# Shared PSUM copies in tiles of their own, and two tap units ahead of the filter's rows, in an SSM convolution with a dense layer

## The chip, the cores and the metric

The kernel runs on one core of one Trainium2 chip. The metric is the device time of one execution in microseconds (us). An execution is also profiled: the trace lists each instruction with its engine, start and duration, and its span runs from the first to the last instruction. The engines are TensorE (PE: matmuls; PEld: its weight loads), VectorE (DVE), ScalarE (ACT), GpSimd (POOL) and SyncE (SP), which only issues transfers. ScalarE issues transfers too, on a queue of its own.

## What is computed

S is 2048 tokens, D is 512 channels, the hidden width is 1376. Cut to what matters:

```python
def _A_ref(q, k, v, shift_k, ssm_k, ssm_D):
    k_pad = jnp.pad(k, ((0, 0), (ks - 1, 0), (0, 0)))
    for t in range(ks):                       # ks = 4 taps per channel
        k_shift = k_shift + k_pad[:, t:t + S, :] * shift_k[:, ks - 1 - t][None, None, :]
    kv = k_shift * v
    y = irfft(rfft(kv, 2S) * rfft(ssm_k, 2S))[:S]       # a long convolution per channel
    y = y + kv * ssm_D
    return q * y

h = x + _A_ref(_layernorm(x), A_k, A_v, A_shift_k, A_ssm_k, A_ssm_D)
h2 = h + relu(_layernorm(h) @ B_w1) @ B_w2
```

## The kernel before

The long convolution is done as a transform in stages of matmuls, of the filter ssm_k and of kv, a product of the two, and the inverse. Then come the gate with q, the layer norm and the dense layer. Everything is written out by hand: each engine executes its instructions in the order of the program, and a helper derives the semaphores. The stages are these.

- **Loads.** SyncE issues the shift weights (wsh, L123), the whole filter ssm_k of 2 MB (tile sk, L124), and then for four pieces of 512 tokens the transposing loads of k and v, k first (L132 to L137). They follow each other in one queue.
- **Fill.** 22 matmuls on zeros (L156) keep TensorE busy until data is there.
- **Tables.** GpSimd makes ramps (iota), two identities (ident in bf16, identw in f32) and a mask; VectorE turns ramps into angles (`_turns`, L44 and L46; tsn, L222 and L220); ScalarE takes sines. ScalarE also makes 16 diagonal matrices wdiag from ident and the shift weights (L204): a matmul with one is a tap. VectorE makes the tables f1hi and f1lo of the first stage (L210 to L215).
- **Rows of the filter.** `to_rows` (L271 to L284) transposes sk on TensorE, 32 transposes in four groups of eight, and copies each group from PSUM into kfl: groups 0 and 2 by ScalarE, group 1 by VectorE, group 3 half by each engine (L281, L283), both from one PSUM tile.
- **Stage 1 of the filter** (`stage1`, L286 to L309): per call 32 pairs of weight load and small matmul into two PSUM tiles. VectorE adds the mask to a half of each (L306) and ScalarE copies the other half (L309).
- **Tap units** (`taps(c, h)`, L329 to L337): eight matmuls with diagonals give the shifted k of 512 tokens and two of the four channel groups; VectorE multiplies by v (L337). One unit stands behind each of the stage calls 0 to 5, two ahead of call 6.
- **Rows of kv** by `to_rows` again, the last stage call of the filter, and eight calls of stage 1 for kv, evicted by both engines (L267, L269).
- **Products** (L425 to L442), and the **inverse** (`inv1`, L550 to L562): 16 blocks of 12 matmuls, each evicted by two copies. ScalarE does most blocks, VectorE blocks 6, 8, 10, 12 and 14, and block 15 is shared half and half, from one PSUM tile. Then `inv2` (L634) writes pz, which the gate reads.
- **The dense layer** (`mlp1`, L646 and L648; `mlp2`, L659 to L665): four groups of four token tiles. Each token tile ends in one product on VectorE (L662) and a store that ScalarE issues (L665).

PSUM tiles of the first stages come in turn from four buffers of two banks each (`bank2`): a tile waits until the one four places before it has been read. A tile that two engines read has its readers ordered one behind the other.

Of the kernel before, what the change touches and what calls it, by code (L numbers as in the profile page):

```python
# [56 lines left out]
def kernel(  # L57
# [64 lines left out]
    wsh = consts.tile([P, DC, KS], BF16, name="wsh")  # L122
    nc.sync.dma_start(out=wsh[:], in_=A_shift_k.rearrange("(r p) j -> p r j", p=P))  # L123
    nc.sync.dma_start(out=sk, in_=A_ssm_k.rearrange("(c p) t -> p c t", p=P))  # L124
    draw = small([DC * P], BF16)
# [14 lines left out]
    nbias = consts.tile([P, 1], F32, name="nbias")  # L140
    pbias = consts.tile([P, 1], F32, name="pbias")
    nc.vector.memset(nbias[:], -0.5 * TURN)
    nc.vector.memset(pbias[:], 0.5 * TURN)
# [13 lines left out]

    fill(bank2("psz")[:, 0, :], 22)

    n1i = early.tile([P, 1], I32, name="n1i")  # L160
    for s in range(0, P, 32):
        nc.gpsimd.iota(n1i[s:s + 32, :], pattern=[[0, 1]], base=0, channel_multiplier=1)
    n2i = consts.tile([P, 1], I32, name="n2i")
    for s in range(0, P, 64):
        nc.gpsimd.iota(n2i[s:s + 64, :], pattern=[[0, 1]], base=0, channel_multiplier=1)
# [4 lines left out]
    f1hi = early.tile([P, 2, 2, 16, 2], BF16, name="f1_hi")  # L170
    f1lo = early.tile([P, 2, 2, 16, 2], BF16, name="f1_lo")
    for f in (f1hi, f1lo):
        nc.gpsimd.memset(f[:], 0.0)
    ident = early.tile([P, P], BF16, name="ident")
    identw = early.tile([P, P], F32, name="identw")
    for t in (identw, ident):
        nc.gpsimd.memset(t[:], 0.0)
        nc.gpsimd.affine_select(out=t[:], in_=t[:], compare_op=ALU.not_equal, fill=1.0,
                                base=0, pattern=[[-1, P]], channel_multiplier=1)
    nc.gpsimd.iota(r2, pattern=[[2, 32], [128, 64]], base=1, channel_multiplier=0)  # L180
    pi4 = consts.tile([P, 2], I32, name="pi4")
# [3 lines left out]
    nc.gpsimd.tensor_copy(out=rows4[:], in_=rows4[:].bitcast(I32))  # L185
    n1c = early.tile([P, 1], F32, name="n1c")
    n2c = consts.tile([P, 1], F32, name="n2c")
    nc.vector.tensor_copy(out=n1c[:], in_=n1i[:])
    nc.vector.tensor_copy(out=n2c[:], in_=n2i[:])
    wf = early.tile([P, DC, KS], F32, name="wf")  # L190
    nc.vector.tensor_copy(out=wf[:], in_=wsh[:])
    t1 = small([64], I32)
    _turns(nc, t1[:, 0:32], r1[:], n1c[:], 128, True)
# [7 lines left out]
    _sin(f1f[:, 32:64], t1[:, 32:64], 128, neg=True)  # L201
    for rg in range(DC):
        for j in range(KS):
            nc.scalar.mul(out=wdiag[:, rg, j, :], in_=ident[:], mul=wf[:, rg, j:j + 1])  # L204
    dsc = small([2, 64], F32)
    dpm = small([2, 64], F32)
    _sin(dsc[:], t3[:], 64)

    f1h = small([64], BF16)
# [7 lines left out]
    st = stp.tile([P, 32, 192], F32R, name="st")  # L217
    def wrap13(t):

        nc.vector.tensor_scalar(out=t, in0=t, scalar1=19, scalar2=19, op0=ALU.logical_shift_left, op1=ALU.arith_shift_right)  # L220

    nc.vector.tensor_single_scalar(out=tsn, in_=r2, scalar=n2c[:], op=ALU.mult)  # L222
    wrap13(tsn)

# [46 lines left out]
    def to_rows(src, h, fl):  # L271

        pst = bank2("pst").rearrange("p b (i c) -> p (b i) c", i=4)
        srcw = src.bitcast(F32).rearrange("p c (a w) -> p (c a) w", w=32)
        for i in range(8):
            nc.tensor.transpose(out=pst[:, i, :], in_=srcw[:, :, 8 * h + i], identity=identw[:])
        o = fl.bitcast(I32)
        for eng, i0, n in {0: (("A", 0, 8),), 1: (("D", 0, 8),), 2: (("A", 0, 8),), 3: (("A", 0, 4), ("D", 4, 4))}[h]:
            oi, pi = o[:, :, 8 * h + i0:8 * h + i0 + n], pst[:, i0:i0 + n, :]
            if eng == "A":  # L280
                nc.scalar.copy(out=oi.bitcast(F32), in_=pi.rearrange("p i c -> p c i"))  # L281
            else:
                nc.vector.tensor_single_scalar(out=oi, in_=pi.bitcast(I32).rearrange("p i c -> p c i"),  # L283
                                               scalar=0, op=ALU.bitwise_or)  # L284
# [43 lines left out]

    def taps(c, h, each=2):  # L329
        ps = bank2("pkv")  # L330
        for i in range(2):
            for j in range(KS):
                nc.tensor.matmul(out=ps[:, i, :], lhsT=wdiag[:, 2 * h + i, j, :],
                                 rhs=kT[c][:, 2 * h + i, 16 - j:CH + 16 - j], start=(j == 0), stop=(j == KS - 1))
        for i in range(0, 2, each):
            vv = vT[:, 2 * h + i:2 * h + i + each, CH * c:CH * c + CH]
            nc.vector.tensor_tensor(out=vv, in0=ps[:, i:i + each, :], in1=vv, op=ALU.mult)  # L337
# [196 lines left out]

    def inv1_mm(b, i, parts):
        g = 4 * b + i
        o = blocks[b][:, i].rearrange("p d a n -> p (d a n)")
        for part in parts:
            src = BX[:, 0] if part == 0 else BK[:, part - 1]
            rhs = inv3[:].rearrange("p d a n -> p (d a n)") if part == 0 else inv12[:, 4 - 2 * part:8 - 2 * part, :].rearrange("p a n -> p (a n)")  # L540
            nc.tensor.matmul(out=o, lhsT=src[:, g // 2, :, g % 2::2].rearrange("p c r -> p (c r)"), rhs=rhs,  # L541
                             start=(part == 0), stop=(part == 2), skip_group_check=True)
# [7 lines left out]
    def inv1(b, eng):  # L550
        if b in blocks:
            for i in range(4):
                inv1_mm(b, i, (0, 1, 2) if i % 2 else (1, 2))
        else:
            blocks[b] = bank2("psi").rearrange("p b (i d a n) -> p (b i) d a n", i=2, d=2, a=2)
            for i in range(4):
                inv1_mm(b, i, (0, 1, 2))
        ps = blocks[b]
        for e, i0, n in ((eng, 0, 4),) if len(eng) == 1 else ((eng[0], 0, 2), (eng[1], 2, 2)):
            for rho in range(2):  # L560
                copy(e, ax[rho][:, :, :, 8 * b + 2 * i0:8 * b + 2 * i0 + 2 * n],
                     ps[:, i0:i0 + n].rearrange("p i d a n -> p a n (i d)")[:, rho].rearrange("p (n m) c -> p n m c", m=2))  # L562

# [10 lines left out]
    for b in range(16):  # L574
        inv1(b, "AD" if b == 15 else "D" if b in (6, 8, 10, 12, 14) else "A")
        if b == 0:
            for n in range(4):
                center(n)
            ec_wrap(1)
            ln1_stats(0)  # L580
        if b == 3:
            ln1_norm(0)
        if b in (8, 9, 10, 11):
            ec_sins(1, (b - 8,))
        if b == 11:
            load_x(1)
# [65 lines left out]
    def mlp2(sc, hook=None):  # L652
        h1T = h1s[sc]
        for i in range(4):
            t = 4 * sc + i
            ps2 = psm.tile([P, D], F32, tag="ps", name="ps2m")
            for fc in range(NFC):
                ksz = min(P, DFF - fc * P)
                nc.tensor.matmul(out=ps2[:], lhsT=h1T[:ksz, fc, i * P:(i + 1) * P], rhs=w2[:ksz, fc, :],  # L659
                                 start=(fc == 0), stop=(fc == NFC - 1))  # L660
            o = ob[t % 3]
            nc.vector.scalar_tensor_tensor(out=o[:], in0=ps2[:], scalar=rstd2[:, t, :], in1=xh[sc][:, i, :],  # L662
                                           op0=ALU.mult, op1=ALU.add)
            dst = bass.AP(tensor=out_d.tensor, offset=out_d.offset + t * D, ap=[[16 * D, 4], [64 * D, 32], [1, D]])
            nc.scalar.dma_start(out=dst, in_=o)  # L665
            if hook is not None:
                hook(i)
# [76 lines left out]
```

## Time and profile before

| what | us |
|---|---|
| median of 3 runs (lowest, highest) | 214.96 (214.94, 216.5) |
| the profiled execution | 214.74 |
| its span | 213.0 |
| TensorE busy | 200.3 |
| VectorE busy | 141.2 |
| ScalarE busy | 115.7 |
| GpSimd busy | 70.3 |

The span is what the rows below cover; the rest of an execution's time lies outside. A row of the time line gives start, duration, engine, line, operation, output and inputs with shapes; in square brackets stand the engine's idle time before the row and what ended it. "SPq" and "ACTq" are transfers being issued: their duration is that of the issue, not of the transfer. A row of the waits gives the engine and line that waited, what it waited for, and us in total, number and longest. The row "PE" of digits divides the span into 40 slices of 5.3 us; a digit is the busy share in tenths.

### The profile page before, as it was taken

To read this page: it belongs to the slowest core of one execution; us is meant where nothing else is said; L and a number is where in the kernel's file an instruction comes from. 1 tells how busy PE (TensorE), PEld (TensorE's weight loads), DVE (VectorE), ACT (ScalarE), POOL (GpSimd) and SP (SyncE) were. 2 spreads that over 40 slices of the span, in tenths; PEclk is the share of its full clock that TensorE was granted. 3 is DMA by queue.
4 is the path that set the end of the run, shared out by engine and by line. 5 is a ranking of instruction groups with operands and counts; after the bars stand their busy time and mean duration, and the time that the engine had idled before them with its cause. 6 is when DMAs were issued, how large, how long until landed. Compare 5 with 4: busy or idle time off the path is not lost. (4 is left out here: it accounts for less than half of the span.)

```text
span 213.0 us, 4286 instructions
## 1 busy us (share of the span) xinstructions
PE 200.3 (94%) x1715; PEld 137.1 (64%) x1724; DVE 141.2 (66%) x243; ACT 115.7 (54%) x186; POOL 70.3 (33%) x119
## 2 busy tenths in 40 slices
PE   7779999999999999999997999999999999999990
PEld 2465555887888888789996954457444844444440
DVE  5978987599678887898743487897078742260121
ACT  3987776687777677657592039501970065026200
POOL 7954703995555893030103022420102110002000
PEclk9999999999999999999999999999999999999997
DMA  5999970001600000037315997999818715110011
GB/s 155 340 219 171 197 118 2 3 5 15 252 3 0 3 0 3 0 99 102 67 32 143 267 210 142 174 170 142 110 33 101 141 24 102 27 57 14 0 51 47
DMA packets 47686, 19.91 MB, mean 93 GB/s; under 512 B 42706, under 2 KB 46132, under 8 KB 47668
## 3 DMA queue, kind: packets, MB, share of 16 engines
q1 hardware_dynamic: 44144, 16.15, 41.1%
q10 hardware_dynamic: 3524, 3.51, 5.6%
q8 instruction: 13, 0.21, 0.5%
q14 instruction: 5, 0.04, 0.1%
HBM read 7.02 MB, written 2.10 MB: 43 GB/s over the span
## 5 line engine op out<-in xcount | busy, mean ns | idle before, releaser
L648 ACT ACTIVATE M<-ps1m 128x512 bf16<-128x512 f32 (+1 forms) x44 | 25.0, 601 | 49.9 <-PE ps1m L646 39.5
L659 PE MATMUL ps2m<-M 128*128 128x512 bf16 (+1 forms) x172 | 38.5, 379 | 0.2
L659 PEld LDWEIGHTS <-M 128*128 128x128 bf16 (+1 forms) x176 | 17.1, 98 | 20.9 <-ACT M L648 0.4
L646 PEld LDWEIGHTS <-w 128*128 128x128 bf16 (+1 forms) x176 | 17.4, 100 | 20.4 <-issue 0.7
L380 POOL TENSOR_TENSOR smc<-st 64x256 fp32r<-64x256 f32 x32 | 22.7, 729 | 11.1 <-PE us L435 10.2
L662 DVE SCALAR_TENSOR_TENSOR M<-ps2m,rstd,M 128x512 bf16<-128x512 f32 x12 | 9.0, 748 | 25.3 <-PE ps2m L659 16.8
L503 POOL TENSOR_SCALAR rstd<-mv 128x4 f32<-128x4 f32 x8 | 2.2, 276 | 70.9 <-DVE mv L501 70.9
L541 PE MATMUL psi<-inv,BK 128*128 128x256 f32 x128 | 22.7, 283 | 0.0
L442 DVE TENSOR_TENSOR BK<-u,ktu 128x512 fp32r<-128x512 f32 x32 | 20.4, 680 | 0.0
L541 PEld LDWEIGHTS psi<-inv,BK 128*128 128x128 f32 x128 | 19.9, 195 | 0.0
L646 PE MATMUL ps1m<-xT,w 128*128 128x512 bf16 (+1 forms) x88 | 19.6, 379 | 0.2 <-ACT M L648 0.2
L646 PE MATMUL ps1m<-M,w 128*128 128x512 bf16 (+1 forms) x88 | 19.3, 379 | 0.0
L541 PE MATMUL psi<-inv,BX 128*128 128x256 f32 x64 | 18.0, 286 | 0.1
L415 ACT COPY ktu<-u 128x512 f32<-128x512 f32 x32 | 17.2, 589 | 1.5
L442 DVE TENSOR_TENSOR BX<-us,kts 128x512 fp32r<-128x512 f32 x16 | 11.1, 691 | 8.4 <-PE u L425 6.7
L415 ACT COPY kts<-us 128x512 f32<-128x512 f32 x16 | 9.4, 587 | 9.5 <-PE us L435 9.5
L425 PE MATMUL u<-BK,st 64*128 64x256 f32 x128 | 14.6, 308 | 0.0
L425 PE MATMUL u<-BX,st 64*128 64x256 f32 x128 | 13.0, 284 | 0.0
L309 ACT CAST BK<-ps 128x512 fp32r<-128x512 f32 x16 | 9.4, 585 | 6.5 <-PE ps L294 3.9
L541 PEld LDWEIGHTS psi<-inv,BX 128*128 128x128 f32 x64 | 12.3, 195 | 0.6 <-DVE BK L442 0.6
L499 DVE BATCH_NORM_STATS2 st<-M 128x6 f32<-128x512 bf16 x20 | 12.3, 677 | 0.0
L435 PE MATMUL us<-BK,smc 128*128 128x256 f32 x64 | 12.0, 310 | 0.0
(127 smaller groups left out, 399.3 us busy)
## 6 DMA issues: line engine op xcount, KB each, us to landing
E<-in_A_ssm_k_dram SPq DMA_DIRECT2D x1, 2048.0 KB
out_dram<-M ACTq DMA_DIRECT2D x16, 128.0 KB
w<-in_B_w_dram SPq DMA_DIRECT2D x1, 1376.0 KB
M<-in_B_w_dram ACTq DMA_DIRECT2D x1, 1280.0 KB
M<-in_A_q_dram SPq DMA_DIRECT2D x8, 128.0 KB
xh<-in_A_q_dram SPq DMA_DIRECT2D x4, 128.0 KB
xr<-in_A_q_dram SPq DMA_DIRECT2D x4, 128.0 KB
M<-in_B_w_dram ACTq DMA_DIRECT2D x1, 96.0 KB
```

Of the source, the lines that this page charges most:

```text
L309: nc.scalar.copy(out=o[1 - rp][:, 1], in_=pv[1 - rp][:, 1])
L380: nc.gpsimd.tensor_tensor(out=smc[pq, c % 4, i, :, 64 * dp:64 * dp + 64], in0=st[pq, ks, 64:128].bitcast(F32), in1=st[pq, ks, 0:64].bitcas ...
L415: nc.scalar.copy(out=kt[:], in_=ps)
L425: nc.tensor.matmul(out=ps[:, dp, 256 * x:256 * x + 256], lhsT=t[pq], rhs=cols((BK, BX)[x], pq, k1, i), start=(i == 0), stop=(i == 1), tile ...
L435: nc.tensor.matmul(out=ps[:, k % 2, 256 * x:256 * x + 256], lhsT=smc[:, k // 4 % 4, i, k % 4, :], rhs=cols((BK, BX)[x], slice(0, P), k, i) ...
L442: nc.vector.tensor_tensor(out=o, in0=ps[:, :, 256:512].rearrange("p b (g x) -> p b g x", x=8), in1=kt[:].rearrange("p b (g x) -> p b g x", ...
L499: nc.vector.bn_stats(out=st[:, i, :], in_=src[:, i, :])
L541: nc.tensor.matmul(out=o, lhsT=src[:, g // 2, :, g % 2::2].rearrange("p c r -> p (c r)"), rhs=rhs, start=(part == 0), stop=(part == 2), sk ...
L646: nc.tensor.matmul(out=ps1[:fsz, :].rearrange("p (i t) -> p i t", i=4), lhsT=w1[:, c, fc * P:fc * P + fsz], rhs=hT[sc][:, :, c, :], start= ...
L648: nc.scalar.activation(out=h1T[:fsz, fc, :], in_=ps1[:fsz, :], func=ACT.Relu)
L659: nc.tensor.matmul(out=ps2[:], lhsT=h1T[:ksz, fc, i * P:(i + 1) * P], rhs=w2[:ksz, fc, :], start=(fc == 0), stop=(fc == NFC - 1))
L662: nc.vector.scalar_tensor_tensor(out=o[:], in0=ps2[:], scalar=rstd2[:, t, :], in1=xh[sc][:, i, :], op0=ALU.mult, op1=ALU.add)
```

## The change

The parts of the change, with the diff below cut to its core:

- The shift weights are loaded by ScalarE's queue, and so is ssm_k, after the first two diagonals that ScalarE makes. SyncE's queue begins with k's first piece. ScalarE does a small sine ahead of that.
- Fifteen fills instead of 22, then two tap units of the first piece, then four fills, then the rows of the filter. The units behind the stage calls become (1,0), (1,1), (2,0) behind calls 0 to 2, none behind call 3, (2,1) behind call 4 and none behind call 5.
- GpSimd makes the long ramp r2 first, then ident; identw and the rest later.
- VectorE makes the diagonals of channel groups 0 and 1, ScalarE those of 2 and 3. tsn and the two tap products stand ahead of f1hi and f1lo on VectorE.
- In `to_rows` the two halves of group 3 have a PSUM tile each, with its own transposes.
- In `inv1` a shared block has a tile for each engine; blocks 14 and 15 are shared, VectorE does 7, 9, 11 and 13.
- The very last token tile is done in two halves of 256 channels, each with its matmuls, product and store.

```diff
-    nc.sync.dma_start(out=wsh[:], in_=A_shift_k.rearrange("(r p) j -> p r j", p=P))
-    nc.sync.dma_start(out=sk, in_=A_ssm_k.rearrange("(c p) t -> p c t", p=P))
+    nc.scalar.dma_start(out=wsh[:], in_=A_shift_k.rearrange("(r p) j -> p r j", p=P))
...
-    fill(bank2("psz")[:, 0, :], 22)
+    psz = bank2("psz")[:, 0, :]
+    fill(psz, 15)
+    nc.gpsimd.iota(r2, pattern=[[2, 32], [128, 64]], base=1, channel_multiplier=0)
+    n2i = consts.tile([P, 1], I32, name="n2i")
...
+    eye(ident)
...
+    nc.scalar.activation(out=nsin[:], in_=nbias[:], func=ACT.Sin)
+    for rg in range(DC):
+        for j in range(KS):
+            if rg < 2:
+                nc.vector.tensor_scalar(out=wdiag[:, rg, j, :], in0=ident[:], scalar1=wf[:, rg, j:j + 1], scalar2=None, op0=ALU.mult)
+            else:
+                nc.scalar.mul(out=wdiag[:, rg, j, :], in_=ident[:], mul=wf[:, rg, j:j + 1])
+            if (rg, j) == (2, 1):
+                nc.scalar.dma_start(out=sk, in_=A_ssm_k.rearrange("(c p) t -> p c t", p=P))
...
+    nc.vector.tensor_single_scalar(out=tsn, in_=r2, scalar=n2c[:], op=ALU.mult)
+    wrap13(tsn)
...
+    taps(0, 0)
+    taps(0, 1)
+    fill(psz, 4)
     f1h = small([64], BF16)
...
-        pst = bank2("pst").rearrange("p b (i c) -> p (b i) c", i=4)
-        for i in range(8):
-            nc.tensor.transpose(out=pst[:, i, :], in_=srcw[:, :, 8 * h + i], identity=identw[:])
-        for eng, i0, n in {0: (("A", 0, 8),), 1: (("D", 0, 8),), 2: (("A", 0, 8),), 3: (("A", 0, 4), ("D", 4, 4))}[h]:
+        for eng, i0, n in {1: (("D", 0, 8),), 3: (("A", 0, 4), ("D", 4, 4))}.get(h, (("A", 0, 8),)):
+            pst = bank2("pst").rearrange("p b (i c) -> p (b i) c", i=4)[:, 0:n]
+            for i in range(n):
+                nc.tensor.transpose(out=pst[:, i, :], in_=srcw[:, :, 8 * h + i0 + i], identity=identw[:])
...
+    behind = {0: (1, 0), 1: (1, 1), 2: (2, 0), 4: (2, 1)}
-        if gb < 6:
-            taps(gb // 2, gb % 2)
+        if gb in behind:
+            taps(*behind[gb])
...
     def inv1(b, eng):
+        n = 4 // len(eng)
+        for i0, e in zip((0, 2), eng):
+            if b not in blocks or i0:
+                blocks[b] = bank2("psi").rearrange("p b (i d a n) -> p (b i) d a n", i=2, d=2, a=2)
+                todo = [(i, (0, 1, 2)) for i in range(n)]
...
-        inv1(b, "AD" if b == 15 else "D" if b in (6, 8, 10, 12, 14) else "A")
+        inv1(b, "AD" if b > 13 else "D" if b in (7, 9, 11, 13) else "A")
...
+            w = D // 2 if t == NT - 1 else D
+            for d0 in range(0, D, w):
+                ps2 = psm.tile([P, D], F32, tag="ps", name="ps2m")[:, 0:w]
+                for fc in range(NFC):
+                    nc.tensor.matmul(out=ps2, lhsT=h1T[:ksz, fc, i * P:(i + 1) * P], rhs=w2[:ksz, fc, d0:d0 + w],
+                                     start=(fc == 0), stop=(fc == NFC - 1))
+                nc.vector.scalar_tensor_tensor(out=o[:, d0:d0 + w], in0=ps2, scalar=rstd2[:, t, :], in1=xh[sc][:, i, d0:d0 + w],
+                                               op0=ALU.mult, op1=ALU.add)
+                nc.scalar.dma_start(out=dst, in_=o[:, d0:d0 + w])
```

More of the change, by code (lines that the diff above doesn't have):

```diff
@@ L141 @@
     pbias = consts.tile([P, 1], F32, name="pbias")
+    nsin = consts.tile([P, 1], F32, name="nsin")
     nc.vector.memset(nbias[:], -0.5 * TURN)
@@ L156, in fill, with eye @@
             nc.tensor.matmul(out=ps, lhsT=zero[:, 0:P], rhs=zero[:], start=True, stop=True, skip_group_check=True)
-    fill(bank2("psz")[:, 0, :], 22)
+    psz = bank2("psz")[:, 0, :]
+    fill(psz, 15)
+    nc.gpsimd.iota(r2, pattern=[[2, 32], [128, 64]], base=1, channel_multiplier=0)
+    n2i = consts.tile([P, 1], I32, name="n2i")
+    for s in range(0, P, 64):
+        nc.gpsimd.iota(n2i[s:s + 64, :], pattern=[[0, 1]], base=0, channel_multiplier=1)
+    f1hi = early.tile([P, 2, 2, 16, 2], BF16, name="f1_hi")
+    f1lo = early.tile([P, 2, 2, 16, 2], BF16, name="f1_lo")
+    ident = early.tile([P, P], BF16, name="ident")
+    identw = early.tile([P, P], F32, name="identw")
+    def eye(t):
+        nc.gpsimd.memset(t[:], 0.0)
+        nc.gpsimd.affine_select(out=t[:], in_=t[:], compare_op=ALU.not_equal, fill=1.0,
+                                base=0, pattern=[[-1, P]], channel_multiplier=1)
+    eye(ident)
     n1i = early.tile([P, 1], I32, name="n1i")
@@ L162 @@
         nc.gpsimd.iota(n1i[s:s + 32, :], pattern=[[0, 1]], base=0, channel_multiplier=1)
-    n2i = consts.tile([P, 1], I32, name="n2i")
-    for s in range(0, P, 64):
-        nc.gpsimd.iota(n2i[s:s + 64, :], pattern=[[0, 1]], base=0, channel_multiplier=1)
     r1 = early.tile([P, 32], I32, name="f1_r")
@@ L169 @@
     nc.gpsimd.iota(r3[:], pattern=[[1, 64]], base=0, channel_multiplier=0)
-    f1hi = early.tile([P, 2, 2, 16, 2], BF16, name="f1_hi")
-    f1lo = early.tile([P, 2, 2, 16, 2], BF16, name="f1_lo")
     for f in (f1hi, f1lo):
         nc.gpsimd.memset(f[:], 0.0)
[L174 to L180, printed above, removed]
+    eye(identw)
     pi4 = consts.tile([P, 2], I32, name="pi4")
@@ L185 @@
     nc.gpsimd.tensor_copy(out=rows4[:], in_=rows4[:].bitcast(I32))
-    n1c = early.tile([P, 1], F32, name="n1c")
     n2c = consts.tile([P, 1], F32, name="n2c")
-    nc.vector.tensor_copy(out=n1c[:], in_=n1i[:])
     nc.vector.tensor_copy(out=n2c[:], in_=n2i[:])
@@ L191 @@
     nc.vector.tensor_copy(out=wf[:], in_=wsh[:])
+    nc.scalar.activation(out=nsin[:], in_=nbias[:], func=ACT.Sin)
[7 more added lines that the diff above has]
+                nc.scalar.dma_start(out=sk, in_=A_ssm_k.rearrange("(c p) t -> p c t", p=P))
+    n1c = early.tile([P, 1], F32, name="n1c")
+    nc.vector.tensor_copy(out=n1c[:], in_=n1i[:])
     t1 = small([64], I32)
@@ L201 @@
     _sin(f1f[:, 32:64], t1[:, 32:64], 128, neg=True)
-    for rg in range(DC):
-        for j in range(KS):
-            nc.scalar.mul(out=wdiag[:, rg, j, :], in_=ident[:], mul=wf[:, rg, j:j + 1])
     dsc = small([2, 64], F32)
@@ L207, with wrap13, taps @@
     _sin(dsc[:], t3[:], 64)
+    st = stp.tile([P, 32, 192], F32R, name="st")
+    def wrap13(t):
+        nc.vector.tensor_scalar(out=t, in0=t, scalar1=19, scalar2=19, op0=ALU.logical_shift_left, op1=ALU.arith_shift_right)
+    nc.vector.tensor_single_scalar(out=tsn, in_=r2, scalar=n2c[:], op=ALU.mult)
+    wrap13(tsn)
+    def taps(c, h, each=2):
+        ps = bank2("pkv")
+        for i in range(2):
+            for j in range(KS):
+                nc.tensor.matmul(out=ps[:, i, :], lhsT=wdiag[:, 2 * h + i, j, :],
+                                 rhs=kT[c][:, 2 * h + i, 16 - j:CH + 16 - j], start=(j == 0), stop=(j == KS - 1))
+        for i in range(0, 2, each):
+            vv = vT[:, 2 * h + i:2 * h + i + each, CH * c:CH * c + CH]
+            nc.vector.tensor_tensor(out=vv, in0=ps[:, i:i + each, :], in1=vv, op=ALU.mult)
+    taps(0, 0)
+    taps(0, 1)
+    fill(psz, 4)
     f1h = small([64], BF16)
@@ L215 @@
             nc.vector.tensor_copy(out=f[rows, :, rg % 2], in_=src[rows, :].rearrange("p (h w v) -> p w v h", h=2, w=2))
[L217 to L223, printed above, removed]
     def big_sin(out, turns, scale):
@@ L271, in to_rows @@
     def to_rows(src, h, fl):
-        pst = bank2("pst").rearrange("p b (i c) -> p (b i) c", i=4)
         srcw = src.bitcast(F32).rearrange("p c (a w) -> p (c a) w", w=32)
-        for i in range(8):
-            nc.tensor.transpose(out=pst[:, i, :], in_=srcw[:, :, 8 * h + i], identity=identw[:])
         o = fl.bitcast(I32)
-        for eng, i0, n in {0: (("A", 0, 8),), 1: (("D", 0, 8),), 2: (("A", 0, 8),), 3: (("A", 0, 4), ("D", 4, 4))}[h]:
-            oi, pi = o[:, :, 8 * h + i0:8 * h + i0 + n], pst[:, i0:i0 + n, :]
+        for eng, i0, n in {1: (("D", 0, 8),), 3: (("A", 0, 4), ("D", 4, 4))}.get(h, (("A", 0, 8),)):
+            pst = bank2("pst").rearrange("p b (i c) -> p (b i) c", i=4)[:, 0:n]
+            for i in range(n):
+                nc.tensor.transpose(out=pst[:, i, :], in_=srcw[:, :, 8 * h + i0 + i], identity=identw[:])
+            oi = o[:, :, 8 * h + i0:8 * h + i0 + n]
             if eng == "A":
-                nc.scalar.copy(out=oi.bitcast(F32), in_=pi.rearrange("p i c -> p c i"))
+                nc.scalar.copy(out=oi.bitcast(F32), in_=pst.rearrange("p i c -> p c i"))
             else:
-                nc.vector.tensor_single_scalar(out=oi, in_=pi.bitcast(I32).rearrange("p i c -> p c i"),
+                nc.vector.tensor_single_scalar(out=oi, in_=pst.bitcast(I32).rearrange("p i c -> p c i"),
                                                scalar=0, op=ALU.bitwise_or)
@@ L327, in more_sines @@
             big_sin(st[:, half, 64:128], r2[:, half], 1)
[L329 to L337, printed above, removed]
     inv3 = consts.tile([P, 2, 2, 64], F32R, name="inv3")
@@ L533, with inv1_mm @@
     blocks = {}
-    def inv1_mm(b, i, parts):
-        g = 4 * b + i
+    def inv1_mm(b, i, parts, i0=0):
+        g = 4 * b + i0 + i
         o = blocks[b][:, i].rearrange("p d a n -> p (d a n)")
@@ L550, in inv1 @@
     def inv1(b, eng):
[L551 to L559, printed above, removed]
+        n = 4 // len(eng)
[3 more added lines that the diff above has]
+                todo = [(i, (0, 1, 2)) for i in range(n)]
+            else:
+                todo = [(i, (0, 1, 2) if i % 2 else (1, 2)) for i in range(n)]
+            for i, parts in todo:
+                inv1_mm(b, i, parts, i0)
             for rho in range(2):
                 copy(e, ax[rho][:, :, :, 8 * b + 2 * i0:8 * b + 2 * i0 + 2 * n],
-                     ps[:, i0:i0 + n].rearrange("p i d a n -> p a n (i d)")[:, rho].rearrange("p (n m) c -> p n m c", m=2))
+                     blocks[b][:, 0:n].rearrange("p i d a n -> p a n (i d)")[:, rho].rearrange("p (n m) c -> p n m c", m=2))
     lift(0)
@@ L655, in mlp2 @@
             t = 4 * sc + i
[L656 to L660, printed above, removed]
-            o = ob[t % 3]
[L662 to L665, printed above, removed]
+            o = ob[t % 3]
+            w = D // 2 if t == NT - 1 else D
+            for d0 in range(0, D, w):
+                ps2 = psm.tile([P, D], F32, tag="ps", name="ps2m")[:, 0:w]
+                for fc in range(NFC):
+                    ksz = min(P, DFF - fc * P)
+                    nc.tensor.matmul(out=ps2, lhsT=h1T[:ksz, fc, i * P:(i + 1) * P], rhs=w2[:ksz, fc, d0:d0 + w],
+                                     start=(fc == 0), stop=(fc == NFC - 1))
+                nc.vector.scalar_tensor_tensor(out=o[:, d0:d0 + w], in0=ps2, scalar=rstd2[:, t, :], in1=xh[sc][:, i, d0:d0 + w],
+                                               op0=ALU.mult, op1=ALU.add)
+                dst = bass.AP(tensor=out_d.tensor, offset=out_d.offset + t * D + d0, ap=[[16 * D, 4], [64 * D, 32], [1, w]])
+                nc.scalar.dma_start(out=dst, in_=o[:, d0:d0 + w])
             if hook is not None:
```

## The prediction

> **What bounds the kernel now.** I read the busy shares first, then TensorE's waits, then the time line wherever a wait stands.
>
> ```profile
> PE 200.3 (94%) x1715; PEld 137.1 (64%) x1724; DVE 141.2 (66%) x243; ACT 115.7 (54%) x186; POOL 70.3 (33%) x119
> PE   7779999999999999999997999999999999999990
> ```
>
> TensorE is busy in 94% of the span; the slices that are not full are the first three and the one near 115 us. What a change can win lies there and in the tail behind the last matmul. TensorE's waits name the same places (us in total, times, longest):
>
> ```profile
> PE ps L294 <- DVE E L283: 1.4, 1, 1.4
> PE pz L634 <- DVE ax L269: 1.4, 1, 1.4
> PE pst L276 <- DMA E<-in_A_ssm_k_dram: 1.3, 1, 1.3
> PE psz L156 <- DVE pbias L143: 1.2, 1, 1.2
> ```
>
> The time line (start us, us) of the front:
>
> ```profile
> 1.25 0.48 SPq L124 DMA_DIRECT2D E<-in_A_ssm_k_dram  x1
> 1.78 7.30 SPq L134 DMA_TRANSPOSE E<-in_A_k_dram  x1
> 3.59 1.93 POOL L180 IOTA G<- 128x2048 int32 x1
> 3.70 1.86 DVE L46 TENSOR_SCALAR E<-E 128x32 int32<-128x32 int32 x1
> 9.13 2.19 SPq L137 DMA_TRANSPOSE E<-in_A_v_dram  x1
> 9.49 3.84 PE L276 MATMUL pst<-identw,E 128*128 128x128 f32 x32 [1.27 <-DMA E<-in_A_ssm_k_dram]
> 12.47 1.50 ACT L281 COPY E<-pst 128x1024 f32<-128x1024 f32 x2 [0.69 <-PE pst L276]
> 14.00 0.69 DVE L283 TENSOR_SCALAR E<-pst 128x512 int32<-128x512 int32 x1 [1.21 <-ACT E L281]
> 15.75 1.90 PE L333 MATMUL pkv<-E 128*128 128x512 bf16 x7
> ```
>
> Nothing real runs on TensorE before 9.49, when ssm_k is there. ScalarE's half of the last row copy ends at 13.97, VectorE's half starts at 14.00 although its transposes ended at 13.33: it waits for ScalarE, on the same tile. The first stage then starts at 14.75, and only from 15.75 does a tap unit fill the array. The second shared copy and the transposes next to another load:
>
> ```profile
> 114.52 0.37 ACT L267 CAST BX<-psi 128x256 fp32r<-128x256 f32 x1 [1.80 <-PE psi L541]
> 115.20 0.42 DVE L269 CAST BX<-psi 128x256 fp32r<-128x256 f32 x1 [0.83 <-ACT ax L267]
> 115.54 0.41 DVE L269 CAST ax<-psi 128x256 fp32r<-128x256 f32 x1
> 116.11 0.36 PE L634 MATMUL pz<-core,BX 128*128 128x256 f32 x1 [1.39 <-DVE ax L269]
> ...
> 117.32 4.79 SPq L507 DMA_TRANSPOSE M<-xr  x1
> ...
> 129.47 1.93 SPq L507 DMA_TRANSPOSE M<-xr  x1
> ```
>
> The same transpose took 1.93 us to issue alone and 4.79 us while the load of w2, issued by ScalarE at 114.53, ran. The load kept its pace: 308 and 306 GB/s in the windows 118 to 119 and 119 to 120.
>
> **The change, part by part.** All against the profiled execution: 214.74 us, span 213.0, so 1.74 lie outside it; the median of the runs is 214.96, 0.22 more.
>
> *1. When ssm_k arrives.* GpSimd now starts with the long iota: 0.82 + 1.93 = 2.75, n2i 0.34, memset and select of ident some 0.6: ident at 3.7. ScalarE issues three small loads (0.46 + 0.81, to 2.0), loads its table (1.28, to 3.3), does one small sine (0.3, the row of L147) and two diagonals of 0.30 (4.77 over 16): the load of ssm_k is issued at 4.3 instead of 1.25. From issue to first transpose it took 9.49 - 1.25 = 8.24: 12.5 undisturbed. It now runs beside k's and v's transposes on the other queue. Nothing here shows a plain load of this size slowed by transposes; the nearest row is w2, which kept its pace, so 0 at one end; the other end is an even split, which doubles the some 5 us in which its packets ran at full pace. I take 0.5: TensorE gets the rows at 13.0, range 12.3 to 17.5.
>
> *2. What TensorE does until then.* 15 fills: weight loads 0.43 apart until 5.42, then 0.21, so 6.5. Two tap units of 1.90: 10.3. Four fills of 0.21: 11.2. Then 1.8 us idle. The first DMA on SP is now k's: issue from 0.72 for some 2.2 (v's rows: 1.97 to 2.19), v's to some 5.1; packets of lone transposes start 1.41 after the issue in the trace's packet records, so k lands near 4.8, before the taps want it at 6.5. If VectorE's memsets are held by the iota as L46 is (1.86 against 0.18 otherwise), the fills start 1.6 later and end at 12.8: still hidden behind the 13.0.
>
> *3. VectorE's queue ahead of the rows.* Eight diagonals at some 0.2 from 3.7 (5.3), nine small operations of 0.2 (7.1; the 1.86 and 1.80 under the iota are gone), tsn 1.36 + 1.23 (9.75), two tap products of 1.22 (12.2), the ten operations of f1 (6.67 to 8.55, so 1.9: 14.1). The second row copy is wanted at 13.0 + 1.92 = 14.9. This holds with 0.8 to spare if v's first piece has landed by 10.5. It is the added wait: f1's tables, two row copies and then TensorE's first stage queue behind those products. Up to 11.1 it stays hidden; beyond it the first stage starts at v's landing + 2.45 + 1.9 + 1.23 + 0.69 + 0.1.
>
> *4. Rows and first stage.* Transposes 13.0 to 16.85; ScalarE's last copy ended 0.64 after them before, VectorE's half now runs beside it: first stage at 17.55. Before it was 14.75, with the 3.80 of the two tap units still to come: 18.55. Gain 1.0.
>
> *5. The stages without taps behind them.* Before, each 0.95 stage has a 1.90 unit behind it (2.85 for TensorE, against 1.28 + 1.22 on VectorE). After, stage 3 has none. Stage 4's second tile then waits for the product of tap unit (2,0): 0.05 + 1.23 - 0.95 = 0.33. Unit (2,1) waits for ScalarE to leave stage 3 (two copies of 0.58 behind VectorE's add): 0.27. Stage 5 waits for stage 4's tile behind a sine of 1.06 and two copies: 0.32. Together 0.9 lost, between 0 (ScalarE idles elsewhere) and 1.4. So stage 6 ends at 17.55 + 21.56 - 3.80 + 0.9 = 36.2, against 36.31: nearly all of step 4 is given back.
>
> *6. The second row copy (near 41).* VectorE waited 1.21 for ScalarE, TensorE 0.42. After the split VectorE's copies of that stage, which follow each other without a gap from 43.34 on, start some 0.35 earlier. Range 0 to 0.43.
>
> *7. The end of the inverse.* The matmuls of block 15 end at 114.49. VectorE's half can start at 114.52 instead of 115.20, and ScalarE's half 0.72 earlier: 0.68. TensorE waited for nothing in the blocks before, so the new sharing of blocks costs 0 as long as four buffers cover it. Range 0.3 to 0.8.
>
> *8. The last tile in two halves.* The last product takes 0.42 (256 wide, L269) instead of 0.75: 0.33. The last store's packets fill four engines for some 1.5 us; half of it, queued behind the first half, may save another 0.3, while 22 instead of 11 weight loads (98 ns each) may cost 0.27. I take 0.4. No row has 512-byte packets: if one costs what a 1024-byte packet does, it is -0.5, at best +0.7.
>
> Sum: 1.0 - 0.9 + 0.35 + 0.68 + 0.4 = 1.5. 214.74 - 1.5 = 213.2, 0.8% under the median.
>
> [...]
>
> **Rivals.**
> *v's first piece late* (0.17). v's issue ends near 5.1 and ssm_k's begins at 4.3: they overlap. If the rest of v waits as the 4.79 transpose did, it lands with ssm_k near 13; the first stage starts at 13 + 6.4 = 19.4, and the sum is 1.85 worse: 215.1. For it: that row; against: most of v is queued before.
> *ssm_k slowed: slower than before* (0.11). One mechanism: the load shares the engines with the transposes of k and v for its whole length. Every us after 13.0 costs one; from 14.5 on the gain is gone, at 17 it is 217.2. Against: the pace of w2. The longest idle stretch of TensorE in this trace is 1.4 us, and the matmuls behind it ran at full pace. [...]
> *Nothing given back* (0.17). ScalarE and VectorE keep up in step 5 and ssm_k is issued while the diagonal still runs: 1.7 - 0.2 + 0.43 + 0.8 + 0.6 = 3.3: 211.4. For it: VectorE idles 0.4 to 0.5 before each tap product.
> *The tap units are no gain at all* (0.05): 214.0, only steps 7 and 8.
>
> **How the numbers follow.** The forecast, 212.2 to 214.3, has 0.50. The 80% range takes in the first and third rival with the bounds around them, 211.2 to 216.0, and leaves out the second. A measurement here tells about 1% from no change: 2.15 us, so faster means under 212.8, slower over 217.1. Faster: 0.17 and a quarter of the forecast, 0.30. Slower: most of the second rival, 0.11. The rest, 0.59, within 1%.
>
> **What would show it.** TensorE's first transpose near 13.0 with the load of ssm_k as its releaser; the first stage near 17.5 (step 4), at 19 or later with VectorE's products waiting for a DMA if v is late; waits of L294 and the taps after stage 3 (step 5); VectorE's half of the shared copies no longer released by ScalarE; pz near 115.4 less what was won before. It is wrong if the row transposes start after 14.5, or if ssm_k is issued later than 5.

## The result and the profile after

The changed kernel takes 218.17 us (median of 19 runs, 216.12 to 221.29), the kernel before 214.8 (19 runs on the same chip, 214.66 to 216.93). The ratio is 1.0115 (95% interval 1.0087 to 1.0144), which leaves out the longest runs, of which the profiled execution, 220.04 us with a span of 218.0, is one. So the change made the kernel 1.2% slower, where 213.2 us, 0.8% faster, was forecast. A second profile of the same kernel, shown further down, has 217.23 and 215.3.

TensorE's waits of the kernel after (us in total, times, longest):

```profile
PE pst L304 <- DMA E<-in_A_ssm_k_dram: 5.6, 1, 5.6
PE psz L156 <- DVE pbias L143: 1.2, 1, 1.2
PE ps L320 <- DVE E L309: 0.9, 1, 0.9
...
PE ps L320 <- ACT BK L335: 0.5, 1, 0.5
PE pst L304 <- PE ps L320: 0.4, 1, 0.4
PE ps1m L663 <- PE pz L651: 0.4, 1, 0.4
```

The wait for ssm_k stands where it stood, now 5.6 us long instead of 1.3, although TensorE now has work until 11.80 in front of it instead of until 8.22. The time line of TensorE up to the rows (start, us):

```profile
1.17 6.30 PE L156 MATMUL psz<-zero 128*128 128x512 bf16 x15 [1.17 <-DVE pbias L143]
7.31 3.62 PE L233 MATMUL pkv<-E 128*128 128x512 bf16 x16
...
17.42 4.77 PE L304 MATMUL pst<-identw,E 128*128 128x128 f32 x27 [5.62 <-DMA E<-in_A_ssm_k_dram]
```

Fills and taps run much as forecast (taps from 7.3, forecast 6.5; TensorE idle from 11.8). The rows start at 17.42, forecast 13.0. The reason begins on the queues, ScalarE's first and then SyncE's:

```profile
3.71 0.69 ACT L201 ACTIVATE E<-ident,wf 128x128 bf16<-128x128 bf16 x2
5.09 0.40 ACTq L204 DMA_DIRECT2D E<-in_A_ssm_k_dram  x1
5.54 1.86 ACT L201 ACTIVATE E<-ident,wf 128x128 bf16<-128x128 bf16 x6 [1.14 <-DMA E<-in_A_k_dram]
```

```profile
2.17 2.55 SPq L136 DMA_TRANSPOSE E<-in_A_v_dram  x1
4.77 2.87 SPq L135 DMA_TRANSPOSE E<-in_A_k_dram  x1
7.68 10.23 SPq L136 DMA_TRANSPOSE E<-in_A_v_dram  x1
```

ScalarE has made its two diagonals by 4.40 and then stands for 1.14 us; the releaser named is a load of k's. The trace's semaphore numbers say which and why: each load counts its arrival on a semaphore (a counter that others wait on), eight of them serve the loads of the front in turn, and ssm_k's load got the one of k's first piece (number 102). The last update for that piece came at 5.07, and the load is issued at 5.09. By then SyncE has begun, at 4.77, to issue k's second piece. The packet records, on the clock of the rows above, show the load's first packet at 7.67, just behind the end of that issue (7.64) and 2.58 us after its own; in the kernel before it came 1.15 us after.

The granted clock is the second thing that no step of the forecast priced. The windows of the kernel after (us; busy time of PE, PEld, DVE, ACT and POOL; PEclk; DMA share; GB/s):

```profile
13.00:14.00 1.00, 0.00 (x0) 0.00 (x0) 0.97 (x1) 0.00 (x0) 0.92 (x1) 0.94 1.06 418
14.00:15.00 1.00, 0.00 (x0) 0.00 (x0) 0.96 (x7) 0.00 (x0) 0.00 (x0) 0.50 1.06 414
...
17.00:18.00 1.00, 0.58 (x3) 0.61 (x4) 0.00 (x0) 0.00 (x0) 0.00 (x0) 0.50 1.26 279
18.00:19.00 1.00, 1.00 (x7) 1.00 (x6) 0.00 (x0) 0.00 (x0) 0.00 (x0) 0.50 1.28 291
```

The clock falls to 0.50 at 13.9, while TensorE is idle, and the row transposes run under it until 20.7. The chain that ended last (start, us) begins with k's first piece, and has the load and then the rows:

```profile
0.72 4.35 DMA E<-in_A_k_dram
5.07 0.02 issue
5.09 12.20 DMA E<-in_A_ssm_k_dram
17.42 5.35 PE pst L304 x32
...
121.44 3.91 PE pz L651 x32
...
213.58 0.48 DVE M L681
```

The 32 transposes take 5.35 instead of 3.84. pz starts at 121.44 (before 116.11).

### The profile page after: what moved, and what is told of

Its sections match the earlier page's. It is cut to its first block, busy times and chain, and to the rows that moved or that the text cites. A ratio compares the mean times of both kernels' runs of the same rounds, so it can differ in the third digit from the quotient of the medians.

```text
span 218.0 us, 4327 instructions
## 1 busy us (share of the span) xinstructions
PE 202.8 (93%) x1732; PEld 139.9 (64%) x1732; DVE 142.1 (65%) x252; ACT 113.7 (52%) x181; POOL 71.3 (33%) x119
## 4 chain that ended last, share of the span: by engine, by line
PE 80%; DMA 8%; DVE 5%; ACT 3%; issue 2%; DVEq 0%
PE ps2m L679 17%; PE ps1m L663 14%; PE psi L558 11%; PE u L442 9%; PE us L452 9%; PE ps L320 7%; DMA E<-in_A_ssm_k_dram 6%; PE pz L651 5%; PE pkv L233 5%; PE pst L304 4%; DMA E<-in_A_k_dram 2%; ACT BX L288 2%; DVE st L516 1%; ACT M L665 1%; DVE qT L637 1%
## 5 line engine op out<-in xcount | busy, mean ns | idle before, releaser
L679 PE MATMUL ps2m<-M 128*128 128x512 bf16 (+3 forms) x187 | 38.8, 366 | 0.0
L679 PEld LDWEIGHTS <-M 128*128 128x128 bf16 (+1 forms) x187 | 18.2, 98 | 20.1 <-ACT M L665 0.4
L681 DVE SCALAR_TENSOR_TENSOR M<-ps2m,rstd,M 128x512 bf16<-128x512 f32 (+1 forms) x13 | 9.2, 707 | 29.0 <-PE ps2m L679 20.5
L304 PE MATMUL pst<-identw,E 128*128 128x128 f32 x64 | 9.2, 311 | 6.1 <-DMA E<-in_A_ssm_k_dram 5.6
L304 PEld LDWEIGHTS pst<-identw,E 128*128 128x128 f32 x64 | 8.8, 201 | 6.7 <-issue 6.1
L558 PEld LDWEIGHTS psi<-inv,BX 128*128 128x128 f32 x64 | 12.3, 195 | 0.6 <-DVE BK L459 0.6
L516 DVE BATCH_NORM_STATS2 st<-M 128x6 f32<-128x512 bf16 x20 | 12.3, 676 | 0.0
```

The costliest lines, as they stand in the source:

```text
L516: nc.vector.bn_stats(out=st[:, i, :], in_=src[:, i, :])
L679: nc.tensor.matmul(out=ps2, lhsT=h1T[:ksz, fc, i * P:(i + 1) * P], rhs=w2[:ksz, fc, d0:d0 + w], start=(fc == 0), stop=(fc == NFC - 1))
```

## The experiments

The theory after the result (A): ssm_k's load comes late because of where it joins the queues: it is issued late, it stands behind the issue of a transposing load (one that transposes on its way, as k's and v's do), and it meets that load's packets; then the clock falls. The rivals: the load is merely late on any queue (B), or the halved clock carries the loss (C).

### The load on SyncE's queue

```diff
         nc.sync.dma_start_transpose(out=vT[:, :, CH * c:CH * c + CH], ...)
+        if c == 0:
+            nc.sync.dma_start(out=sk, in_=A_ssm_k.rearrange(...))
...
-            if (rg, j) == (2, 1):
-                nc.scalar.dma_start(out=sk, in_=A_ssm_k.rearrange(...))
```

> The changed kernel, but ssm_k's load is issued on SyncE's queue, right behind k's and v's first pieces, instead of on ScalarE's. Theory A (the load lost its time where its packets met the transposes of k's and v's second pieces on another queue: almost no packet ended between 8.5 and 11.9): in one queue they cannot meet, v's packets end near 6.7 and the load's 5.1 us follow, so TensorE gets the rows between 12.2 and 13.0, the clock stays full, the first stage starts near 17.2 and the time is 212.5 to 213.5. Rival B (a load that starts behind transposes is slow on any queue, or is simply late): rows at 16 or later, time 216 to 218.

Measured: 214.8 us (214.51 to 218.15, 10 runs), ratio 1.0 (0.9971 to 1.0029), span 212.5. Issued at 4.59, first packet at 5.95, rows at 13.44, transposes at the full clock behind 2.2 us of idle time. All of the loss is gone with the place of one load; the change's gain is not there either. The load also has a free semaphore here and waits for none, so this run alone does not part the late issue from the meeting on the queues.

### k's second piece held back until ssm_k has landed

```diff
-    for c in range(4): ... k's and v's pieces
+    k's and v's piece 0
...
+    nc.gpsimd.tensor_copy(out=kT[1][:, 0, 0:1], in_=sk[:, 0, 0:1])
+    for c in range(1, 4): ... k's and v's pieces
```

> The changed kernel with ssm_k still on ScalarE's queue, but the transposes from k's second piece on wait until ssm_k has landed (a one-column copy on GpSimd from ssm_k's tile into k's second tile makes them wait; it changes nothing of the result, since the transpose writes over it). Theory A: no transpose is in flight beside the load after v's first piece, so the load takes some 8.2 us from its issue at 4.4 to 5.1: rows at 12.6 to 13.4, time 213 to 214 if k's second piece still comes in time for the tap unit behind stage 0. Rival B: rows at 16 or later, 217 or more.

Measured: 215.26 us (215.12 to 216.66, 10 runs), ratio 1.0005 (0.9976 to 1.0035), span 213.3. With fewer loads ahead of it the load found a free semaphore: issued at 3.72, rows at 12.94. So the load is not bound to be late on ScalarE's queue, though its first packet again came 2.94 us behind the issue, 1.43 behind the end of the issue of v's first piece (5.23). The later pieces cost on the other side: a product of VectorE waited 1.7 for v's second piece, ScalarE's copy for VectorE, and TensorE 1.0 for that copy.

### The copies and the tail alone

The kernel before, with only `to_rows`, `inv1` and the last tile as in the changed one.

> The kernel before with only the later parts of the change: own tiles for the shared copies of the rows and of the inverse with the new sharing of blocks, and the last token tile in two halves; the front (loads, fills, taps, diagonals) stays as before. By the prediction's steps 4 (its copy part, 0.65), 6 (0.35), 7 (0.68) and 8 (0.4): 2.1 us less, 212.7. Rival: in the changed kernel these parts are swallowed by VectorE and ScalarE, and nothing shows: 214.3 to 214.8.

Measured: 213.02 us (212.97 to 213.16, 4 runs), ratio 0.9892 (0.9846 to 0.9939): the fastest kernel of the study. TensorE's waits of this kernel:

```profile
PE ps L294 <- DVE E L283: 0.9, 1, 0.9
PE pz L634 <- DVE ax L269: 0.5, 1, 0.5
PE ps L294 <- ACT BK L309: 0.5, 1, 0.5
```

The two waits of 1.4 of the kernel before have become 0.9 and 0.5. The third line is new: the kernel before waits 0.4 at that place for VectorE's half of kv's rows, this one 0.5 for ScalarE's copies. The half's own tile takes one more of the four buffers in turn, so a later tile has to wait for a buffer. Step 6 gains nothing. The first shared copy's own tile is worth 0.4 here (kv's rows start at 36.52 instead of 36.91), where the run expected 0.65.

### Fills up to the rows

`fill(psz, 4)` behind the tap units becomes `fill(psz, 30)`.

> The changed kernel with 30 instead of 4 fills behind the first two tap units, which keeps TensorE busy until near 16.5. Rival C (the clock: TensorE idle for 5.6 us came back at half pace and the 32 row transposes took 5.35 instead of 3.84): 1.5 us less than the changed kernel when the load lands at the same time, so 216 to 217, and less spread between runs. Theory A alone (the clock costs nothing that is not hidden): as the changed kernel, 217 to 219.

Measured: 217.44 us (216.94 to 219.42, 4 runs), ratio 1.0114 (1.0046 to 1.0182), span 215.1. The load's last packet ended at 14.71; the fills themselves held the rows to 16.15. Rows to first stage took 4.63 at the full clock, against 6.21 in the profile of the changed kernel. The experiment was spoilt by its own size; it is done better further down.

### ssm_D's two small loads made one

```diff
-    for dp in range(2):
-        src = bass.AP(tensor=A_ssm_D.tensor, offset=A_ssm_D.offset, ap=[[0, 1], [1, DC * P]])
-        nc.scalar.dma_start(out=draw[64 * dp:64 * dp + 1, :], in_=src)
+    src = bass.AP(tensor=A_ssm_D.tensor, offset=A_ssm_D.offset, ap=[[0, 2], [1, DC * P]])
+    nc.scalar.dma_start(out=draw[0:65:64, :], in_=src)
```

> The changed kernel, but ssm_D's two small loads are one, so that ssm_k's load does not share a completion semaphore with a load that is still open. If the wait for that semaphore is the whole of the late arrival: issued near 3.7 instead of 5.1, rows some 8.2 to 8.7 later, 12 to 12.5, as step 1 of the prediction had it, and 214.0 to 214.8 us. If meeting the transposes of the other queue is the cause: issued near 3.7 as well, but its first packet 2.3 to 3.1 us behind the issue instead of 1.4, rows at 13 to 16, 215 to 218 us, and as wide a spread from run to run as the changed kernel has (216 to 221).

Measured: 214.24 us (213.59 to 216.3, 10 runs), ratio 0.9984 (0.995 to 1.0019), span 211.7 in a run of 213.59. Its time line, queues and rows:

```profile
3.72 0.38 ACTq L203 DMA_DIRECT2D E<-in_A_ssm_k_dram  x1
```

```profile
2.15 3.04 SPq L135 DMA_TRANSPOSE E<-in_A_v_dram  x1
5.24 5.43 SPq L134 DMA_TRANSPOSE E<-in_A_k_dram  x1
```

```profile
13.02 3.84 PE L303 MATMUL pst<-identw,E 128*128 128x128 f32 x32 [1.25 <-DMA E<-in_A_ssm_k_dram]
```

One load fewer ahead of it, and ssm_k's turn falls on the semaphore of the shift weights, which landed at 2.79. It is issued at 3.72, ahead of k's second piece instead of behind it. Now it is k's issue that takes long (5.43), and the rows start at 13.02, where the forecast had them. The first packet still came 2.71 us behind the issue, 1.25 behind the end of the issue of v's first piece (5.19). And v's first piece, whose last packets now share the engines with the load, landed only at 10.23; VectorE's products waited for it:

```profile
10.32 2.36 DVE L236 TENSOR_TENSOR E<-pkv,E 128x1024 bf16<-128x1024 f32 x2 [0.46 <-DMA E<-in_A_v_dram]
```

Six of the ten runs lie at 213.6 to 214.4, the others at 215.6 to 216.3. That is no sign that something of the meeting is left: the kernel before scatters about as far beside them (214.61 to 216.51 in 17 runs).

### The load beside k's first piece

ScalarE issues ssm_k's load right behind the shift weights'.

> The changed kernel, but ScalarE issues ssm_k's load right behind the small first one, near 1.2, so that it starts together with k's first piece on SP's queue. If two queues that both have work disturb each other from the start: first packet over 2 us after the issue, rows at 10 to 13 or k's and v's first pieces late with the taps behind them, 213.5 to 217 us. If only the late issue costs: rows ready near 9.5, before the taps end at 11.2, first stage near 16 (VectorE's queue bounds it), 212.3 to 213 us.

Measured: 217.46 us (216.95 to 218.33, 4 runs), ratio 1.0116 (1.0075 to 1.0156). The waits of TensorE begin with

```profile
PE pkv L231 <- DMA E<-in_A_k_dram: 4.7, 1, 4.7
```

ssm_k's packets ran from 3.15 to 10.23, 7.1 us where they took 6.4 in the kernel before, and k's first piece, which lands at 5.07 in the changed kernel, landed at 11.2. Where the two met here, it was the transposing load that gave way.

### The copies and the tail, with the load first

The kernel of the copies and the tail, where ScalarE issues the shift weights' load so that ssm_k's is SyncE's first.

> The kernel before with the shared copies in tiles of their own and the last tile in halves, and SP's first issue is ssm_k's load (the 0.48 of the small load in front of it goes to ScalarE). If the rows hang on this one load from its issue on, everything up to the last product moves by 0.48 to 0.53: rows at 9.0, first stage at 13.9, 212.5 us, ratio 0.988. If the fills or the diagonals bound the start instead, 213.0 us as without it.

Measured: 219.23 us (218.39 to 219.87, 6 runs), ratio 1.0188 (1.0153 to 1.0223). This is a miss that shows something. VectorE's time line of this kernel:

```profile
9.36 0.17 DVE L191 CAST wf<-wsh 128x16 f32<-128x16 bf16 x1 [7.28 <-DMA wsh<-in_A_shift_k_dram]
```

ssm_k was indeed there at 9.26. But the shift weights, 4 KB issued on the other queue at about the same time, landed at 9.3, with the last of ssm_k. They are 512 packets of 8 bytes beside ssm_k's 512 of 4096 bytes, and the chain that ended last has them for 8.61 us, from 0.73 on; in the kernel before, issued 0.5 us ahead of it, they are used at 2.90. The diagonals, the tables and the row copies all hang on them, and TensorE then waits 4.0 us for VectorE.

### The rest of the front, with the load first

The changed kernel with ssm_k's load as SyncE's first, 22 fills and the tap units behind the stages.

> The changed kernel with ssm_k's load as SP's first issue and the tap units back behind the stages; what stays of its front is GpSimd's new order, the diagonals by two engines and the small sine. If these are worth nothing by themselves once the load leads: rows at 9.0, 212.5 us, the same as the kernel before with the split copies and the load first. If GpSimd's later tables are missed or the diagonals are in VectorE's way: rows or first stage 0.3 to 1 later, 212.8 to 213.5 us. If the tail of the first sines and diagonals was in the way before: 212.0 us.

Measured: 219.8 us (218.91 to 220.24, 6 runs), ratio 1.0219 (1.0182 to 1.0255). The shift weights were late here too: ScalarE's diagonals waited for them until 9.42. What GpSimd's order and the shared diagonals are worth by themselves stays open.

### The changed kernel once more

> The changed kernel once more, for a second profile. Its own runs spread from 216 to 221 us. If the stall of the load where it meets the transposes comes and goes, the rows start anywhere between 14.3 (5.1 + 9.2, the time from issue to rows of the runs without a stall) and 17.5, and the time follows: 216 to 217 us with the early end, 220 with the late one. If the stall is fixed, rows at 17.4 and 220 us again.

Measured: 217.71 us (217.23 to 220.45, 4 runs), ratio 1.0162 (1.0069 to 1.0255). The profiled run has 217.23 us, span 215.3:

```profile
5.48 0.41 ACTq L204 DMA_DIRECT2D E<-in_A_ssm_k_dram  x1
5.94 1.86 ACT L201 ACTIVATE E<-ident,wf 128x128 bf16<-128x128 bf16 x6 [1.54 <-DMA E<-in_A_k_dram]
```

```profile
14.74 5.36 PE L304 MATMUL pst<-identw,E 128*128 128x128 f32 x32 [4.23 <-DMA E<-in_A_ssm_k_dram]
```

The wait for the semaphore (1.54), the place behind k's second piece (issued 5.23 to 7.54; first packet 7.65) and the halved clock are there again. The stall is not: no packet of ssm_k took over 0.74 us, while the first profile has 15 of over 1 us, up to 3.72, all begun where the two loads met (8.0 to 8.2) and ended at 11.4 to 11.7; the transposes' packets nearly stopped as well. The stall comes and goes, and with it 2.7 us.

### Sixteen fills behind the tap units

> The changed kernel with 16 fills instead of 4 behind the two tap units (0.2 each, to some 13.7), so that TensorE's idle time before the rows is shorter by 2.5. If the halved clock costs 1.5 of the loss: the row transposes take 3.84 at the full clock, rows to first stage 4.7 instead of 6.2, and the fastest runs are at 214.7 instead of 216.1; with a stall of the load the clock may still fall. If the clock costs nothing: 216 to 221 us, median 218, as the changed kernel.

Measured: 215.9 us (215.79 to 220.48, 10 runs), ratio 1.0046 (1.0027 to 1.0065), span 213.8.

```profile
14.77 3.84 PE L304 MATMUL pst<-identw,E 128*128 128x128 f32 x32 [1.69 <-DMA E<-in_A_ssm_k_dram]
```

This is the cleanest pair of the study. The rows are there at the same time as in the run before (14.77 and 14.74), TensorE was idle for 1.69 instead of 4.23, the transposes take 3.84 instead of 5.36, and the span is 1.5 shorter. In these two profiles the clock costs 1.5 (the medians of the two runs are 1.8 apart). The rows still start too late, and the fastest run, 215.79, is not at the 214.7 expected.

### The load issued behind the last diagonal

As the run with ssm_D's loads in one, with `(rg, j) == (3, 3)` as the place of the issue.

> As the run with ssm_D's loads in one, but ssm_k's load issued behind ScalarE's last diagonal, near 5.9, where it needs no semaphore that is still open. If only the moment of the issue counts, whatever it waited for: rows 9.3 behind it, at 15.2 or later, the clock halved by the idle time, 217 to 220 us. If the semaphore wait was what hurt: rows at 13.0 + 2.2 at most 15.2, first packet 1.4 behind the issue, 215 us or less.

Measured: 216.61 us (214.33 to 220.46, 10 runs), ratio 1.0041 (0.9999 to 1.0083). The profiled run, 214.35 us:

```profile
5.28 0.41 ACTq L203 DMA_DIRECT2D E<-in_A_ssm_k_dram  x1
```

```profile
5.23 5.11 SPq L134 DMA_TRANSPOSE E<-in_A_k_dram  x1
```

The load again has the semaphore of k's first piece, against what was expected: that piece's last update came at 5.26. Issued at 5.28, close to the 5.09 of the changed kernel, and yet the first packet ran at 6.44, 1.16 behind the issue as in the kernel before, and the rows started at 13.71. So neither expectation held: the moment alone does not decide, nor does the semaphore wait alone. In this run the issue came 0.05 us behind the start of that of k's second piece and still went ahead of it; in the four profiles where it came 0.25 to 0.32 behind, the first packet came only 0.03 to 0.15 behind the end of that issue. That the runs of this kernel scatter over 6 us would fit an order that falls now one way and now the other; this was the author's estimate, since only one of them was profiled.

### The tap units in halves

As the run with ssm_D's loads in one; the four units behind the stages become eight halves, one ahead of the first stage and 1, 1, 1, 2, 1, 1 behind the six.

> As the run with ssm_D's loads in one, but the four tap units left for the stages are cut into eight halves of 0.95: one ahead of the first stage, in the 0.9 that TensorE waits for VectorE's row copy, and 1, 1, 1, 2, 1, 1 behind the six stages. If step 5 is right (a stage without taps behind it costs 0.3 because ScalarE and VectorE need longer for it than TensorE), stage 6 starts 0.9 to 1.6 earlier than the 35.6 of that run and the time falls to 212.6 to 213.3 us. If the stages are bound by ScalarE's and VectorE's sum instead, stage 6 stays at 35.3 to 35.6 and the time at 214 us.

Measured: 215.61 us (215.03 to 217.79, 10 runs), ratio 1.0025 (0.9991 to 1.0059). In the profiled run the load stalled (14 packets of over 1 us) and the rows started at 13.98 at a clock that fell soon after, so its span is not compared. Within it, from the first stage to stage 6 took 19.38, with one half fewer in it than the 17.81 of whole units. Its waits:

```profile
PE ps L319 <- ACT BK L334: 2.4, 5, 1.0
```

Each half takes a buffer of its own, and stages now wait five times for ScalarE to empty one. The halves take away no wait; they add some.

## Why the prediction was wrong

The time fell out of the range on the slow side. The front of the kernel in five spans (us), which also closes the sum:

| | rows start | row transposes | first stage | second rows | span |
|---|---|---|---|---|---|
| forecast | 13.0 | 3.85 | 17.55 | 36.6 | 211.5 |
| one load of ssm_D | 13.02 | 3.84 | 17.73 | 37.04 | 211.7 |
| changed, 16 fills | 14.77 | 3.84 | 19.48 | 38.78 | 213.8 |
| changed, second profile | 14.74 | 5.36 | 20.97 | 40.27 | 215.3 |
| changed, first profile | 17.42 | 5.35 | 23.63 | 42.93 | 218.0 |

The forecast's 36.6 is its end of stage 6, 36.2, and the 0.43 wait of the kernel before; its span is 213.2 less 1.74. Here "second rows" is the start of kv's rows. From the second line to the fourth: 1.72 for the rows, 1.5 for the clock, and 0.4 for the wait of ps1m for pz that the listing after shows, together 3.6. To the fifth: 2.7 more for the stall.

**Step 1 failed**: "the load of ssm_k is issued at 4.3", and the 0.5 for what it meets. The issue was at 5.09 and 5.48, since it had to wait until k's first piece, which had the same semaphore, had landed (5.07 and 5.46). The working went through ScalarE's instructions one by one and did not count the loads that are open when it issues. From issue to rows it took 9.1 to 9.3 us in two profiles of the changed front without a stall, and 12.3 with it, where the kernel before took 8.24 and the forecast 8.74: the first packet came 1.9 to 2.6 us behind the issue instead of 1.15, behind the other queue's issue. The forecast's own 1.41 for lone transposes reads 1.17 to 1.18 on the clock of the rows. With two small loads merged the rows start within 0.02 of the forecast, but that is partly luck: the issue did not wait for the diagonals and came 0.58 earlier than the 4.3 of the working, and the way to the rows was 0.56 longer.

**The mechanism that was named and set aside was the right place.** The rival "ssm_k slowed" had the slow side and 217.2 us, but for another reason: that the load shares its engines with the transposes. It does not lose by that. In the first profile, from 12.0 to 14.5, 48 packets of ssm_k and 48 of the transposes started in each half microsecond, one for one: 16 of each in 0.17 us, of 159 ns and 18 ns. That is nearly what ssm_k gets alone in the kernel before (49 to 54). The row of w2, on which the forecast leaned, said just this, and it held. What that row could not show is a start: w2's load was under way when the transpose joined. The other end of step 1, an even split that doubles the time of the load's packets, was not seen in these 2.5 us either.

**The clock** had no term in the sum; the kernel before shows it at 1.00 behind its longest idle time of 1.4 us. In the profiles of the changed kernel and its variants, idle times of 2.2 and 2.3 us left it whole, and behind 3.3, 4.2 and 5.6 it stood at half. How long after the beginning of the idle time it fell differs: 4.2 us in the second profile, 2.1 us in the first (more on this in the last section). It cost 1.5.

**Step 2** held: fills to 7.3, taps to 10.9, fills to 11.8 (forecast 11.2).

**Step 3** held in its result. v's first piece was in time in the changed kernel: the two products start at 9.77. With the load issued early it was only just so: it landed at 10.23, where the step allowed 10.5, so the first rival, a late v, came close. VectorE's tables ended at 15.4 instead of 14.1, since a cast stood 1.85 us beside GpSimd; with the rows at 13.02 the row copies behind them were 0.2 late in all.

**Step 4**: rows to first stage 4.71 at the full clock (forecast 4.55). Against the break-even of 18.55 the gain is 0.82 with the rows at 13.02; with the rows at 14.74 and the clock halved it is a loss of 2.4.

**Step 5** held: from the first stage to stage 6 the kernel before takes 20.66, less 3.80 for two units 16.86; after it is 17.81, so 0.95 is lost (forecast 0.9). That uncovered stages are the whole reason is not shown: spreading the units in halves brought nothing back.

**Steps 6 and 7**: from the second rows to pz 79.20 before, 78.51 with the copies alone: 0.69 for both. It all belongs to step 7 (0.68 forecast): the blocks' last matmul ends 77.58 after the second rows before and 77.57 with the copies alone; and step 6 is 0 instead of 0.35, because the wait for VectorE became a wait for a buffer.

**Step 8**: 0.4 forecast, 0.69 measured with the copies and the tail alone: 0.16 from pz to the end of the last product, and 0.53 from there to the end of the span (4.43 before, 3.90).

The sum for the kernel in which step 1 holds: 0.82 - 0.95 + 0 + 0.67 + 0.72 = 1.26, the last two measured in that run, and its span is 1.3 shorter than that before. The forecast was 1.5. So the terms behind the load were about right, and the front earned nothing even then: what the two units ahead of the rows gain, the stages behind them give back.

**The range** had the rows at up to 17.5 in its working, and then left that end out with a chance of 0.11. A load that has never been issued from that queue, beside those loads, was the one unknown of the sum, and the range should have taken it in.

**Left open**: what makes the stall of up to 3.7 us that comes in some runs soon after the load's packets and the transposes have met (at 8.0 in the first profile, at 9.5 to 11.3 in the run with half units). Why the load's first packet follows the end of the other queue's issue is not shown either; the profiles show only that it does.

## What to carry to other kernels

When a load is moved, count the loads that are still open when it is issued and whether it must wait for one of their semaphores, and look what the other queue is issuing at that moment: in eight profiles here the first packet came only behind the end of that issue, 1.9 to 2.9 us behind its own. Beside small-packet transfers the large load here nearly kept its pace (7.1 us instead of 6.4) and they were late (k's first piece at 11.2 instead of 5.07), so put what is small and wanted early ahead of it, not beside it. Ahead of the wait here, sixteen fills left TensorE idle for 1.69 us and kept the clock (transposes 3.84), and four, with 4.23 us idle, did not (5.36). Work moved ahead of a wait earns only what the stages it was taken from do not need; the two sure gains here (a tile of its own for each reader, a last tile in halves) were worth 1.8 us alone and were drowned by the front.

## What the runs showed of the hardware

- In the first profile of the changed kernel, from 12.0 to 14.5, two loads on two queues went packet by packet: 48 of 4096 bytes and 48 of 256 bytes started in each half microsecond, so the packets were shared evenly and not the bytes. Loads of many small packets came late beside ssm_k: k's first piece landed at 11.2 instead of 5.07, and a load of 4 KB in 512 packets at 9.3 instead of before 2.9.
- The first packet of ssm_k's load came 1.13 to 1.36 us behind its issue where the other queue was issuing no transposing load (five profiles). It came 1.9 to 2.9 us behind it in eight profiles where the other queue was issuing one, each time behind the end of that issue, by 0.03 to 1.43 us. In one profile, issued 0.05 us behind the start of such an issue, it went ahead, after 1.16.
- The granted clock stood at 0.50 for 6.83 us in the first profile of the changed kernel (13.89 to 20.72), for 3.41 in its second (14.71 to 18.12) and for 3.41 in the run with half units (15.01 to 18.42). In the 3.41 us ahead of the fall TensorE was busy, by the profile's rows, for 39%, 0% and 30%. So the clock did not fall at a fixed time after TensorE became idle, and it fell on work that had begun again: in the run with half units the rows started at 13.98, after 3.3 us of idle time, and the clock went to half 1.0 us later. It stayed whole over the idle times of 2.2 and 2.3 us of the runs with the load on SyncE's queue and behind the last diagonal; in the kernel before it stayed whole for 204.8 us, over idle times of up to 1.4 us, and fell at 210.3, 2.6 us behind the last matmul. What sets the moment of the fall is not shown.
